# Three real products for a complex one in all four frequency classes of a fused spectral filter and feed-forward kernel, with two butterfly buffers placed in the tags of later ones

## The chip, the cores and the metric

The kernel runs on one core of one Trainium2 chip. The metric is the device time of one execution in microseconds, as the median of several runs. A profiled execution gives the page and the trace that are read here; it has a time of its own.

## The reference, cut to what matters

```python
def reference(A_x, A_w_r, A_w_i, B_x, B_w1, B_w2):
    xn = _layernorm(A_x)                       # (1, 2048, 1024)
    X  = rfft2(xn)                             # 2048 x 513, complex
    s  = irfft2(X * (A_w_r + 1j * A_w_i))      # the spectral filter
    h  = silu(xn @ B_w1)                       # 1024 -> 3584
    g  = silu(h @ B_w2)                        # 3584 -> 1024
    return A_x + s * g
```

All inputs and the output are fp32. The feed-forward part is by far the larger one in multiplications; the two-dimensional transform, the filter and the transform back run beside it.

## The kernel before, in words

**Numbers in two halves.** Every factor of a matmul is split into a high and a low fp16 half, and every product is made as three passes: high by high, high by low, low by high. VectorE and ScalarE make these halves: a ScalarE copy with a scale gives the high half, a VectorE `scalar_tensor_tensor` the low one.

**The big matmuls.** `mm1` (L457) makes one chunk of 128 hidden features by 512 rows with 24 matmuls of 512 columns. There are 112 such chunks. ScalarE takes each result out of PSUM with a SiLU (L475), and `hidden` (L481) splits four of them at a time into halves that go to DRAM. The second product is written as seven products of half size (`PRODUCTS`); its chunks are `mm2` (L545, 42 matmuls of up to 512 columns), eight for each of the seven. Results of both lie in the PSUM pool `pf`, which has four buffers of one bank.

**The transform beside it.** It is cut into pieces that are taken from a queue `bg` between the chunks:

- `fd_gen` (four classes c of rows): `fa_mat` transforms along the 1024 columns, `fa_evac` copies to SBUF, `bfly` makes butterflies on VectorE in tiles `E`, `EE`, `EO`, `DS`, `P` and `Q`. Then, in four steps j, a radix-4 step over the rows (tiles `Rb`, `Rd`, `Ro`) and a split into halves in a tile `Rs`, which goes to DRAM as `vd`. For the frequency classes in `THREE` the sum of real and imaginary part (`total`, tile `vt` in tag `E`) is split too and goes to DRAM as `vs`.
- `f_gen` (16 units u; q = u // 4 is the frequency class, j = u % 4 the block of 128 columns): `mat` finishes the transform along the rows with the tables `kq`. For a class that is not in `THREE` it makes four groups of 9 matmuls into one PSUM tile `fx`: three passes of one matmul with 256 columns (L1001) and two with 128 (L1002, L1003). For a class in `THREE` it makes 36 matmuls with 128 columns (L994) into two PSUM tiles: one group multiplies the sum from `vs`, two multiply the real and the imaginary part from `vd`. `copy` then moves one part to SBUF on ScalarE (L1027, one copy into tile `xc`; or L1024, two copies, each laid out twice, into tile `xo` in tag `T1`). For a class in `THREE` two VectorE additions (L1056) join the three products. After that every unit is alike: butterflies `xb`, `xd`, `X`, the product with the weights `wq` (tiles `T1`, `T2`), `yb`, `yd`, `Z`, a split into `zq`, and a store to `zd`.
- `i_gen` (four classes, in the order 1, 3, 0, 2) makes the transform back; its results (`s`, for the last class `rows`) are used by the last steps of the second product.

**PSUM for the transform.** `fa`, `fx`, `iu` and `id` share the pool `pt`, tag `ft`, which has two buffers of two banks each.

**What sets the order.** The program writes the order of each engine's work by hand. After each chunk `after` runs the evacuations that are due (`settle`), delayed stores (`tick`), and `work`, which takes pieces from the queues: weights (`wq`), maxima (`xq`), and the transform (`bg`). A piece of `bg` is taken only while a running estimate of VectorE's time, made from the shapes of the instructions, is no more than `LEAD` = 1.0 us ahead of the same estimate for TensorE. So more VectorE work in `bg` moves later pieces to later chunks. A generator that yields `PAUSE` waits for the next chunk. The last four chunks of `mm1` take nothing from `bg` (`hold`), and when 15 chunks are left `f_job`, which ends the forward transform and opens the pool of `f_gen`, is finished in any case (L1604 to L1607).

**Queues.** Loads and stores are issued from the queue of SyncE (SP), in program order; `load_h` of the second product and the later tables `kq` from ScalarE's queue; the adding loads of `w2` (L424) and the first table from GpSimd's.

The lines of the change:

```python
THREE = (2, 3)                                                              # L28
room = ap.tile([128, 2048 + 256 * len(THREE)], F16, ..., tag="Rs", bufs=2)  # L882
total[j] = ap.tile([128, len(THREE), 128], F32, ..., tag="E", bufs=1)       # L907
load_s(u + 2)                                                               # L1061
```

## Time and profile before

| | |
|---|---|
| median of 3 runs | 1225.4 us (1224.5 to 1226.07) |
| profiled execution, its own time | 1228.22 us |
| its span | 1226.4 us |
| TensorE, VectorE, ScalarE busy | 99%, 82%, 40% of the span |
| instructions | 19138 |
| moved by DMA | 299.98 MB |

The span runs from the first to the last instruction; the own time is 1.8 us longer. In the rows that follow, PE is TensorE's matmuls, PEld its weight loads, DVE is VectorE, ACT ScalarE, POOL GpSimd, and SPq the queue of SyncE. A matmul's duration runs from its start to its modelled end and overlaps with that of the next one, so its cost is read from the distance between starts. The stages can be told by time: the forward transform runs to about 532 us, the 16 units of the filter from 552 to 843 us, `mm2` from 636 us to the end, and the transform back from 880 to 1172 us.

### The profile page before, as it was taken

What the parts mean: (1) busy time and instruction counts of PE and PEld (TensorE: products, weight loads), DVE (VectorE), ACT (ScalarE), POOL (GpSimd) and SP (SyncE); (2) the same over time, 40 slices, a digit from 0 to 9 for tenths busy, and PEclk for the clock granted to TensorE, in tenths of its full rate; (3) what the DMA queues carried; (4) which work ended last, traced back from release to release, by engine and by line L of the source; (5) the groups of instructions that cost most, each with busy time, mean ns of one, the idle gap of its engine ahead of it and who ended that gap; (6) DMA issues with size and microseconds to landing.
All of it is one profiled execution on the core that took longest, in us unless ns stands there. A gap on an engine that the chain in (4) does not pass through costs nothing.

```text
span 1226.4 us, 19138 instructions
## 1 busy us (share of the span) xinstructions
PE 1213.9 (99%) x6992; PEld 616.3 (50%) x6992; DVE 1004.1 (82%) x2007; ACT 494.7 (40%) x670; POOL 137.0 (11%) x255
## 2 busy tenths in 40 slices
PE   8999999999999999999999999999999999999998
PEld 5544445445444444445445555544555555455545
DVE  7778997898798798868968989895378976897766
ACT  6775553455375654434433222131132322333212
POOL 3320000002000000201101121142101111000000
PEclk9999999999999999999999999999999999999999
DMA  8887585747678978479998999987979999997677
GB/s 251 184 195 188 164 256 178 211 132 211 187 257 270 315 242 273 146 245 212 174 294 289 256 256 231 313 227 230 287 188 322 268 344 295 320 368 244 234 246 278
DMA packets 285055, 299.98 MB, mean 245 GB/s; under 512 B 48928, under 2 KB 211744, under 8 KB 284576
## 3 DMA queue, kind: packets, MB, share of 16 engines
q1 hardware_dynamic: 264944, 239.95, 67.1%
q10 hardware_dynamic: 15840, 50.67, 11.9%
q0 software_dynamic: 4176, 8.13, 3.6%
q8 instruction: 55, 0.90, 0.3%
q14 instruction: 40, 0.33, 0.1%
HBM read 188.05 MB, written 104.35 MB: 238 GB/s over the span
## 4 chain that ended last, share of the span: by engine, by line
PE 69%; DMA 10%; DVE 10%; ACT 3%; issue 2%; SPq 1%; POOL 0%; ACTq 0%; DVEq 0%; POOLq 0%
PE pa L466 33%; PE pb L549 10%; PE pb L550 10%; PE pb L551 10%; DMA zd<-zq 2%; PE id L1371 2%; DMA ht<-hd_dif 2%; DMA wq<-in_A_w_i_dram 1%; ACT xp L750 1%; DMA jr<-ws 1%; DMA jr<-in_B_w_dram 1%; PE iu L1289 1%; DMA ws<-wd 1%; PE iu L1281 1%; DVE wd L383 1%
## 5 line engine op out<-in xcount | busy, mean ns | idle before, releaser
L466 PE MATMUL pa<-xnT,w 128*128 128x512 f16 x2688 | 584.4, 379 | 1.3 <-ACT w L257 0.7
L466 PEld LDWEIGHTS <-w 128*128 128x128 f16 x2688 | 261.2, 98 | 312.5 <-issue 1.2
L549 PE MATMUL pb<-w,ht 128*128 128x512 f16 (+2 forms) x812 | 301.1, 373 | 0.0
L550 PE MATMUL pb<-w,ht 128*128 128x512 f16 (+2 forms) x812 | 301.0, 372 | 0.0
L551 PE MATMUL pb<-w,ht 128*128 128x512 f16 (+2 forms) x812 | 300.8, 372 | 0.0
L551 PEld LDWEIGHTS <-ht 128*128 128x128 f16 x812 | 79.6, 98 | 91.4 <-issue 0.8
L549 PEld LDWEIGHTS <-ht 128*128 128x128 f16 x812 | 79.8, 98 | 87.2 <-issue 0.8
L550 PEld LDWEIGHTS <-ht 128*128 128x128 f16 x812 | 79.6, 98 | 87.1 <-issue 0.6
L475 ACT ACTIVATE h<-pa,s 128x512 f32<-128x512 f32 x112 | 75.5, 677 | 76.7 <-PE pa L466 59.5
L257 ACT ACTIVATE w<-jr,sc 128x512 f16<-128x512 f32 x98 | 68.5, 714 | 76.1 <-DMA jr<-in_B_w_dram 57.2
L260 DVE SCALAR_TENSOR_TENSOR w<-jr,sc,w 128x512 f16<-128x512 f32 x98 | 71.9, 744 | 17.9 <-ACT w L257 17.8
L257 ACT ACTIVATE hosum<-hr,hs 128x1536 f16<-128x1536 f32 x28 | 44.0, 1572 | 87.4 <-DVE hr L505 37.5
L260 DVE SCALAR_TENSOR_TENSOR hoone<-h,hs,hoone 128x2048 f16<-128x2048 f32 x28 | 65.6, 2342 | 6.9 <-ACT hoone L257 6.9
L257 ACT ACTIVATE hoone<-h,hs 128x2048 f16<-128x2048 f32 x28 | 55.9, 1995 | 29.3 <-issue 11.8
L260 DVE SCALAR_TENSOR_TENSOR hosum<-hr,hs,hosum 128x1536 f16<-128x1536 f32 x28 | 50.7, 1811 | 1.4 <-ACT hosum L257 1.4
L504 DVE TENSOR_TENSOR hr<-h 128x1024 f32<-128x1024 f32 x28 | 34.1, 1219 | 21.3 <-ACT h L475 21.3
L257 ACT ACTIVATE w<-w1r,rs 128x1024 f16<-128x1024 f32 x28 | 31.9, 1143 | 37.5 <-DVE w L260 24.3
L424 POOL DMA_DIRECT2D jr<-in_B_w_dram x28 | 24.4, 948 | 181.5 <-DMA jr<-in_B_w_dram 43.7
L642 ACT ACTIVATE pl<-pl,c 128x512 f32<-128x512 f32 (+2 forms) x28 | 17.7, 656 | 66.3 <-DVE pl L618 36.5
L1033 ACT ACTIVATE zq<-Z,zs 128x1024 f16<-128x1024 f32 x16 | 18.4, 1148 | 58.5 <-DVE Z L1124 28.9
L1124 POOL TENSOR_TENSOR Z<-yb 128x32 f32<-128x32 f32 x32 | 15.9, 517 | 209.9 <-DVE yb L1103 209.9
L260 DVE SCALAR_TENSOR_TENSOR w<-w1r,rs,w 128x1024 f16<-128x1024 f32 x28 | 35.6, 1273 | 2.3 <-ACT w L257 2.2
(240 smaller groups left out, 1571.5 us busy)
## 6 DMA issues: line engine op xcount, KB each, us to landing
w1r<-in_B_w_dram SPq DMA_DIRECT2D x28, 512.0 KB, 6.7
hd_sum<-hosum SPq DMA_DIRECT2D x56, 256.0 KB, 2.9
hd_one<-hoone SPq DMA_DIRECT2D x56, 256.0 KB, 4.3
hd_dif<-hoone SPq DMA_DIRECT2D x56, 256.0 KB, 4.5
w2m<-in_B_w_dram SPq DMA_DIRECT2D x28, 512.0 KB, 6.1
ht<-hd_dif ACTq DMA_DIRECT2D x32, 448.0 KB, 8.1
jr<-in_B_w_dram SPq DMA_DIRECT2D x56, 256.0 KB, 7.7
ht<-hd_sum ACTq DMA_DIRECT2D x32, 448.0 KB, 5.5
```

The costliest lines, as they stand in the source:

```text
L257: nc.scalar.activation(hi, raw, AF.Copy, scale=scale)
L260: nc.vector.scalar_tensor_tensor(lo, raw, scale, hi, op0=OP.mult, op1=OP.subtract)
L424: nc.gpsimd.dma_start(raw[n], w2_block(*todo[n], 1), accum_op=OP.add)
L466: nc.tensor.matmul(ps, w[:, wh, d], xt[:, xh, d], start=(n == 0), stop=(n == 23))
L475: nc.scalar.activation(hq[:, 2 * (c % 2) + f % 2], ps, AF.Silu, scale=s1[:, f:f + 1])
L504: tt(sums[:, 0:2], hq[:, 0::2], hq[:, 1::2], op=OP.subtract)
L549: nc.tensor.matmul(ps, hh[:, 0], w[:, 0], start=first, stop=False)
L550: nc.tensor.matmul(ps, hh[:, 0], w[:, 1], start=False, stop=False)
L551: nc.tensor.matmul(ps, hh[:, 1], w[:, 0], start=False, stop=last)
L642: nc.scalar.activation(o, o, AF.Silu, scale=c2)
L1033: nc.scalar.activation(zqs[q][:, 0, :, 16 * j:16 * j + 16], zs_[u], AF.Copy, scale=zs)
L1371: nc.tensor.matmul(ps[:, g, cols], us[g][:, uh, 4 * r + p], C["ci"][:, ch, g, r, cols], start=(r == 0 and n == 0), stop=(r == 1 and n == 2 ...
```

## The change

`THREE` becomes (0, 1, 2, 3), so that classes 0 and 1 (units 0 to 7) are made in the way that classes 2 and 3 were. What follows from the constant: the tables of classes 0 and 1 hold cos and two sums instead of sines and cosines (the same size); `total` has four classes instead of two in each of the 16 steps of the forward transform, its two halves are 512 elements per partition instead of 256, and each store of `vs` has 256 KB instead of 128; `Rs` has 3072 fp16 elements per partition instead of 2560, in two buffers. Units 0 to 7 load `vs` too, and the first two of these loads are written out ahead of the loop. The tile `xc` of the plain form is no longer made; `vs` of the filter uses its tag. The butterfly tiles `P` and `Q` lose tags of their own (1040 bytes per partition each) and lie in the tags `Rb` and `Rd` (2048 bytes each), which the radix-4 step uses later in the same class.

```diff
-THREE = (2, 3)
+THREE = (0, 1, 2, 3)
...
             tt(ds[:, 1], o[:, 1], o[:, 3], op=OP.add)
-            pp = ap.tile([128, 4, 65], F32, name=f"P{c}_{p}", tag="P", bufs=1)
+            pp = ap.tile([128, 4, 65], F32, name=f"P{c}_{p}", tag="Rb", bufs=1)
             tt(pp[:, 0:4:3], o[:, 0], o[:, 2, ::-1], op=OP.add)
             tt(pp[:, 2:0:-1], o[:, 0], o[:, 2, ::-1], op=OP.subtract)
-            qq = ap.tile([128, 4, 65], F32, name=f"Q{c}_{p}", tag="Q", bufs=1)
+            qq = ap.tile([128, 4, 65], F32, name=f"Q{c}_{p}", tag="Rd", bufs=1)
...
         load_k(0)
         yield PAUSE
         load_v(0)
+        load_s(0)
         load_w(0)
         yield PAUSE
         yield PAUSE
         load_v(1)
+        load_s(1)
         load_w(1)
         load_k(1)
```

## The prediction

> **What bounds the kernel now.** I read the page's first part, then the waits of TensorE, then the order in time of the matmuls around the change, then the groups by shape and the busy time by stage.
>
> ```profile
> span 1226.4 us, 19138 instructions
> PE 1213.9 (99%) x6992; PEld 616.3 (50%) x6992; DVE 1004.1 (82%) x2007; ACT 494.7 (40%) x670; POOL 137.0 (11%) x255
> ```
>
> PE is busy but for 12.5 us. Its whole list of waits, with the total, the times and the longest, is this:
>
> ```profile
> PE tp L759 <- ACT x L750: 2.1, 3, 1.2
> PE fa L803 <- ACT L L813: 1.9, 1, 1.9
> PE eps L1161 <- POOL edge L1154: 1.1, 1, 1.1
> PE spin L1545 <- POOL ones L1537: 1.0, 1, 1.0
> PE pa L466 <- ACT w L257: 0.7, 1, 0.7
> PE pa L466 <- DMA xnT<-xs: 0.6, 1, 0.6
> PE tp L759 <- DVE xnT L767: 0.3, 1, 0.3
> ```
>
> These are 7.7 us in an execution of 1226.4 us, most of the rest lies before the first and after the last matmul, and no `fx` (the filter's product) and no `pb` (the second product) is in the list. PE could still be called busy while its instructions only overlap, so the starts must be looked at. The timeline of PE around unit 0, in the old form, and around unit 8, in the form that the change gives to all:
>
> ```profile
> 552.59 0.27 PE L1001 MATMUL fx<-vq,kq 128*128 128x256 f16 x1
> 552.70 0.22 PE L1002 MATMUL fx<-vq,kq 128*128 128x128 f16 x1
> 552.76 0.22 PE L1003 MATMUL fx<-vq,kq 128*128 128x128 f16 x1
> 552.81 0.27 PE L1001 MATMUL fx<-vq,kq 128*128 128x256 f16 x1
> ...
> 555.24 5.13 PE L466 MATMUL pa<-xnT,w 128*128 128x512 f16 x23
> ```
>
> ```profile
> 700.70 0.33 PE L994 MATMUL fx<-vs,kq 128*128 128x128 f16 x3
> 700.87 0.50 PE L994 MATMUL fx<-vq,kq 128*128 128x128 f16 x6
> ...
> 702.71 0.38 PE L549 MATMUL pb<-w,ht 128*128 128x512 f16 x1
> ```
>
> A matmul of 256 columns is followed after 0.11 us, one of 128 after 0.055. Nothing lies between the unit and the big matmuls on either side. PE streams without a hole here, so a column less is time less, as long as nobody makes PE wait.
>
> That is where the Trainium skill speaks against this change: Perfetto Trace Analysis, section Identifying the Most-Contended Engine, says that the share of matmul busy time is no measure of TensorE's headroom and that weight loads and the other engines' occupancy should be looked at. By that rule the 50% of PEld stand against DVE's 82%, DVE is the most contended engine, and the change moves work to it. The starts above say otherwise for PE, and a rival below holds what would follow if they didn't.
>
> **What is removed.** A unit in the old form takes 555.24 - 552.59 = 2.65 us of PE, in the new one 702.71 - 700.70 = 2.01 us: as many matmuls (36) and weight loads, but 4608 columns in place of 6144. The difference of 0.64 us times 8 units is **5.1 us of PE**. It is the only saving that counts. On ACT one copy of 592 ns goes per unit, for two others.
>
> **What is added.** The groups by shape, with busy time, mean ns and the idle time before:
>
> ```profile
> L994 PE MATMUL fx<-vq,kq 128*128 128x128 f16 x192 | 15.9, 219 | 0.0
> ...
> L1056 DVE TENSOR_TENSOR xo<-xo,fx 128x512 f32<-128x512 f32 x16 | 10.2, 674 | 0.0
> ...
> L1024 ACT ACTIVATE xo<-fx 128x512 f32<-128x512 f32 x16 | 8.7, 596 | 60.1 <-DVE yd L1104 49.8 <-DMA jr<-in_B_w_dram 10.2
> ...
> L909 DVE TENSOR_TENSOR vt<-Ro 128x256 f32<-128x256 f32 x16 | 6.8, 425 | 0.5
> ...
> L890 DVE SCALAR_TENSOR_TENSOR Rs<-vt,Rs 128x256 f16<-128x256 f32 x16 | 6.7, 418 | 0.0
> ...
> L884 ACT ACTIVATE Rs<-vt 128x256 f16<-128x256 f32 x16 | 6.5, 407 | 9.9 <-DVE vt L909 9.9
> ...
> L1027 ACT ACTIVATE xc<-fx 128x512 f32<-128x512 f32 x8 | 4.7, 592 | 13.6 <-PE fx L1003 8.1 <-issue 5.5
> ```
>
> *Forward transform.* L909, L890 and L884 go from 256 to 512 elements in each of 16 steps. No row has L909 at 512; L1056 has an addition of that size at 674 ns, 249 more, and I take the same step for L890 (its bounds: nothing and another 418). DVE: 16 x (0.249 + 0.249) = 8.0 us. ACT: at most to the 596 of L1024, 16 x 0.19 = 3.0 us.
>
> *Filter.* Units 0 to 7 get two additions each, 8 x 2 x 0.674 = 10.8 us of DVE, and on ACT 8 x (2 x 0.596 - 0.592) = 4.8 us. Together **18.8 us of DVE and 7.8 us of ACT**. Whether they cost anything depends on the room:
>
> ```profile
> 420.00:540.00 120.00, 120.00 (x578) 55.14 (x577) 106.73 (x213) 59.87 (x75) 10.86 (x9) 1.00 0.73 226
> 540.00:690.00 150.00, 150.00 (x872) 77.66 (x870) 123.03 (x188) 57.41 (x71) 13.12 (x26) 1.00 0.96 247
> 690.00:840.00 150.00, 148.84 (x920) 77.81 (x918) 138.60 (x252) 37.13 (x56) 38.95 (x87) 0.99 0.90 248
> ```
>
> The columns after the length are PE, PEld, DVE, ACT and POOL busy, the granted clock, DMA's share and GB/s. In 420 to 540 us DVE has 13.3 us free, in 540 to 690 us 27, against the 10.8 that units 0 to 7 bring there. And where there is no room, the estimate of DVE's time in the program's order puts the next piece of the transform behind a later chunk of big matmuls: PE's own work does not wait for it, the transform ends later. How much later may that be? Its last product and the first use of it by the second product:
>
> ```profile
> L633 DVE SCALAR_TENSOR_TENSOR pl<-rows,s_sc,pl x12: 345/614/752, 1200.8 to 1223.1; 128x512 f32<-128x512 f32 x6, 128x128 f32<-128x128 f32 x4, 128x256 f32<-128x256 f32 x2
> ...
> L1418 DVE SCALAR_TENSOR_TENSOR rows<-sk,spa x4: 283/288/292, 1154.3 to 1171.8; 128x128 f32<-128x128 f32 x4
> ```
>
> The first block of `rows` is ready at 1154.6 and used at 1200.8, the last at 1172.1 and used in the last 22 us. If all 18.8 us of DVE delayed it and PE came 5.1 us earlier, 24 of these 46 us would be gone. Cost: nothing. Without that cover every further microsecond would be paid in full, after the last matmul.
>
> *PSUM.* A unit in the new form takes both buffers of the pool that the transform's matmuls share, so the next unit's matmuls wait until L1056 has read the unit before. Units 8 to 15 run so already, and L994 has an idle time of 0.0. For units 0 to 7 I take 0; the nearest stall of this kind (PE at L803, waiting for ACT to clear that pool) is 1.9 us, once.
>
> *Loads and stores.* The issue rows (operation, count, size, median us from issue to landing):
>
> ```profile
> vs<-Rs SPq DMA_DIRECT2D x16, 128.0 KB, 5.4
> vs<-vs SPq DMA_DIRECT2D x8, 256.0 KB, 10.6
> ```
>
> 16 stores grow by 128 KB and 8 loads of 256 KB come new: 2.1 MB each way, 9 us of DMA traffic at the 226 to 247 GB/s of those stages. A load of unit u + 2 is issued a whole unit ahead, and must then wait only for the matmuls of unit u, like the `vq` load behind it; queued behind it on SP are the stores of hidden features and the loads of `w2`. The share of 0.96 between 540 and 690 us says that these will land later. PE waited for no `ht` and only 0.7 us for a weight, so I take 0, and up to 1 us if it gets twice as long.
>
> *The shared tags.* `P` and `Q` are written and read by DVE alone, and so are `Rb` and `Rd`. A new use stands behind the old one in the same queue: 0, and nothing to be gained.
>
> **Sum.** 5.1 us less on PE, all else covered: the profiled execution goes from 1228.22 to 1223.1 us (span 1221.3). The median of the runs is 2.8 us below the profiled one; the same saving puts it from 1225.4 to **1220.3 us**.
>
> **The rivals.** *A larger gain.* Other timing can take away the waits at L803 and L1161. The latter costs more than its 1.1 us. An undisturbed stretch of the chain that ended last, and PE's timeline right after that wait:
>
> ```profile
> 443.90 41.46 PE pa L466 x192
> ```
>
> ```profile
> 809.47 0.63 PE L550 MATMUL pb<-w,ht 128*128 128x512 f16 x1
> ...
> 812.03 0.52 PE L550 MATMUL pb<-w,ht 128*128 128x512 f16 x1
> ```
>
> In the first a matmul of 512 columns starts each 41.46 / 192 = 0.216 us. In the second six such steps take 2.56 us, 0.43 each, half that rate; 6 x 0.21 = 1.3 us are lost. With all three gone the time is 1220.3 - 1.9 - 1.1 - 1.3 = 1216.0 us. For it speaks only that the pieces shift; 12%.
>
> The Trainium skill, TensorE: Matmul & The Clock Gate, section What's actually happening, has the clock halved only after an idle window of about 3.4 us. By that rule a new wait shorter than that would cost its own length alone; by the rows above a wait of 1.1 us among small matmuls was followed by half the rate, so I count 1.3 us more.
>
> *No change.* The forward transform is where ACT and DVE already make PE wait. If each of the starts of its classes 1, 2 and 3 has a wait like the one of 1.9 us, 3.8 us come new, and with one spell of half the rate 5.1: 1225.4 us. The idle time of 13.3 us on DVE speaks against it. 14%, and another 1% for the case that units 0 to 7 run as before: the code branches on `THREE` alone, so I see no way to it.
>
> *Slower.* In the old form ACT's copy of a unit waits for PE (L1027: 8.1 us); in the new one it writes into the tag of `T1` and must wait until DVE has done `yd` of the unit before (L1024: 49.8 us, over 8 units 6.2 each). For units 8 to 15 ACT has little else to do. Units 1 to 4 run in the first product, where ACT's queue holds the SiLU behind that copy, and with it PE's four buffers. How near is that? ACT's timeline, and PE's:
>
> ```profile
> 612.58 0.67 ACT L475 ACTIVATE h<-pa,s 128x512 f32<-128x512 f32 x1
> ...
> 614.37 0.67 ACT L475 ACTIVATE h<-pa,s 128x512 f32<-128x512 f32 x1
> 615.19 0.69 ACT L475 ACTIVATE h<-pa,s 128x512 f32<-128x512 f32 x1 [0.15 <-PE pa L466]
> ```
>
> ```profile
> 604.63 17.64 PE L466 MATMUL pa<-xnT,w 128*128 128x512 f16 x81
> ```
>
> The third evacuation waited for the chunk that ended at 615.0, the second of the row from 604.63 on (24 matmuls, 5.18 us each chunk). So the first one, done at 613.25, is of the chunk before that row, and its buffer is wanted by the fourth chunk of it, at 604.63 + 3 x 5.18 = 620.2: 6.9 us to spare. A hold of 6.2 + 0.6 us by a copy just fits. The rival decides from 8.8 us a copy on, where four copies cost 1.9 us each and eat the 5.1 and 2.5 more. With 13 us for two of them it gives 1220.3 + 2 x 6.1 = 1232.5 us. Against it: right behind the copy ACT waits for a still later DVE instruction anyway (`Z`, for `zq`). 13%.
>
> *DVE as the bound* (what the page's rule above would lead to): the 18.8 us of DVE come on top and PE's saving turns into waiting, 1225.4 + 18.8 = 1244.2 us. Against it stand the 222 us in which DVE is idle, and PE's short list of waits. 6%.
>
> **How the numbers follow.** The forecast has 54%; its own range is one wait like L803's more or less, 1218.4 to 1222.2 us. 0.2% or 2.5 us is about what a measurement of this kernel can tell from no change. Faster by more: forecast and larger gain, 0.66. Within: 0.15. Slower: 0.13 + 0.06 = 0.19. The range reaches down to the larger gain, 1216.0, and up half the way from no change to the slower rival, (1225.4 + 1232.5) / 2 = 1229.0; left out are about half of that rival and the bound DVE, some 13%.
>
> **What would show it.** Right: L1001 to L1003 and L1027 gone, L994 with 576 matmuls in 16 units of 2.01 us, PE busy 5 us less, L1056 and L1024 with 32, DVE busy 17 to 20 us more, PE's waits still under 10 us in all, the last `rows` some 10 to 20 us later. Wrong: waits of PE at `pa` for L475 or at `fx` for L1056, half-rate spells, or `rows` later than their use.

## The result, and the profile after

The changed kernel takes **1243.87 us** (median of 5 runs, 1241.88 to 1246.09) where the kernel before takes 1226.07 (5 runs on the same chip): a ratio of **1.0136**, 95% interval 1.0119 to 1.0154. It is slower by some 17 us; 5 us faster was forecast. The profiled execution took 1241.88 us, its span is 1240.1 us, 13.7 more than the span before. It was the fastest of its five, and the profiled execution before lies 2.2 us above the 1226.07, so the two traces show 13.7 of the 17 us. The lines of the page that answer to those of before:

```profile
span 1240.1 us, 19155 instructions
PE 1213.8 (98%) x6992; PEld 615.0 (50%) x6992; DVE 1021.5 (82%) x2023; ACT 500.8 (40%) x678; POOL 133.5 (11%) x255
```

VectorE has 17.4 us more work and ScalarE 6.1, near the 18.8 and 7.8 expected. But PE busy is 1213.8 us as before, where 5 us less were expected. The groups by shape (busy, mean ns, idle before) say that the work itself is what the prediction counted:

```profile
L994 PE MATMUL fx<-vq,kq 128*128 128x128 f16 x384 | 32.6, 222 | 0.0
L994 PE MATMUL fx<-vs,kq 128*128 128x128 f16 x192 | 21.5, 221 | 4.2 <-DVE xo L1058 4.2
L1058 DVE TENSOR_TENSOR xo<-xo,fx 128x512 f32<-128x512 f32 x32 | 20.4, 678 | 7.0 <-ACT xo L1026 7.0
L1026 ACT ACTIVATE xo<-fx 128x512 f32<-128x512 f32 x32 | 17.4, 595 | 97.1 <-DVE yd L1106 97.1
L909 DVE TENSOR_TENSOR vt<-Ro 128x512 f32<-128x512 f32 x16 | 11.1, 692 | 0.5
```

There are 576 matmuls at L994 and none in the old form. What has grown is the time in which TensorE stands. Its waits (total, times, longest), those of 1 us and more after the start of the kernel:

```profile
PE iu L1291 <- DVE ub L1300: 4.7, 1, 4.7
PE fx L994 <- DVE xo L1058: 4.2, 2, 3.1
PE eps L1163 <- POOL edge L1156: 2.6, 1, 2.6
...
PE pb L549 <- DMA ht<-hd_dif: 1.6, 1, 1.6
PE fa L803 <- ACT L L813: 1.4, 1, 1.4
PE pa L466 <- ACT h L475: 1.2, 2, 1.0
```

In the list of before there was none of `iu`, `fx` or `pb`, and `eps` had 1.1 us. And by stage (PE, PEld, DVE, ACT, POOL busy, granted clock, DMA share, GB/s):

```profile
540.00:690.00 150.00, 147.78 (x870) 74.32 (x868) 119.38 (x179) 58.89 (x76) 14.88 (x23) 1.00 0.94 246
690.00:840.00 150.00, 142.59 (x865) 75.01 (x863) 133.27 (x242) 37.35 (x55) 20.01 (x50) 0.97 0.98 262
```

PE had 148.84 of 150 us in the second stage before and has 142.59 now. In the first, DVE is busy for 119.38 us where it was 123.03, although it has more to do: the work was not put into the idle time that was counted for it, but moved behind it.

**A balance.** For this and the runs below I worked out from all 6992 matmuls of a trace where TensorE's time goes. Each gets the distance that its shape keeps in undisturbed stretches (0.216 us for 512 columns, 0.109 for 256, 0.056 for 128, small ones in proportion, four times that in fp32). What the next one starts later than that is lost, be it a wait or half the rate; some 6 us of the span lie ahead of the first and after the last matmul. The executions in the table lie up to 3 us from the median of their kernel, so it accounts for their own spans. In us:

| kernel (profiled execution) | matmuls' own time | lost 0–540 | 540–700 | 700–870 | 870–end | span |
|---|---|---|---|---|---|---|
| before | 1208.0 | 7.5 | 0.0 | 4.7 | 0.4 | 1226.4 |
| after | 1202.9 | 6.1 | 2.6 | 14.6 | 8.2 | 1240.1 |
| forward part alone | 1208.0 | 6.3 | 0.3 | 8.9 | 0.4 | 1229.9 |
| products alone | 1202.9 | 6.8 | 0.0 | 7.9 | 5.9 | 1229.4 |
| old work, new order | 1208.0 | 6.7 | 0.0 | 4.3 | 11.3 | 1236.3 |
| new work, old order | 1202.9 | 7.5 | 11.9 | 12.3 | 0.4 | 1240.8 |
| products, old order | 1202.9 | 6.1 | 7.3 | 8.4 | 0.4 | 1231.1 |
| short products, one buffer | 1202.9 | 6.6 | 2.9 | 10.4 | 0.4 | 1229.1 |

The matmuls' own time falls by the 5.1 us, from 1208.0 to 1202.9, as it must with these distances and the new shapes. Against it stand 9.9 us more lost between 700 and 870 us, 7.8 after that and 2.6 before, less 1.4 at the start: 18.9 - 5.1 = 13.8, the 13.7 us of the spans but for rounding. PE busy hides the saving: at half the rate a matmul of 512 columns starts each 0.43 us in place of 0.216, still without a gap, so the longer stretch counts as busy throughout.

### The profile page after: what moved, and what is told of

Its sections match the earlier page's. It is cut to its first block, busy times and chain, and to the rows that moved or that the text cites. A ratio compares the mean times of both kernels' runs of the same rounds, so it can differ in the third digit from the quotient of the medians.

```text
span 1240.1 us, 19155 instructions
## 1 busy us (share of the span) xinstructions
PE 1213.8 (98%) x6992; PEld 615.0 (50%) x6992; DVE 1021.5 (82%) x2023; ACT 500.8 (40%) x678; POOL 133.5 (11%) x255
## 2 busy tenths in 40 slices
DMA packets 290303, 304.17 MB, mean 245 GB/s; under 512 B 49056, under 2 KB 215968, under 8 KB 289824
## 4 chain that ended last, share of the span: by engine, by line
PE 45%; DMA 21%; DVE 19%; ACT 4%; issue 4%; SPq 2%; ACTq 0%; DVEq 0%; POOL 0%; POOLq 0%
PE pa L466 27%; PE pb L549 5%; PE pb L551 5%; PE pb L550 5%; DMA jr<-in_B_w_dram 3%; DMA zd<-zq 2%; DMA ht<-hd_dif 2%; DVE w L260 2%; DVE Z L1126 2%; DMA jr<-ws 2%; PE id L1373 1%; DMA hd_dif<-hoone 1%; DMA vq<-vd 1%; DMA ht<-hd_sum_d 1%; ACT xp L750 1%
## 5 line engine op out<-in xcount | busy, mean ns | idle before, releaser
L475 ACT ACTIVATE h<-pa,s 128x512 f32<-128x512 f32 x112 | 75.1, 675 | 46.0 <-PE pa L466 34.6
L257 ACT ACTIVATE hoone<-h,hs 128x2048 f16<-128x2048 f32 x28 | 55.9, 1996 | 38.1 <-DVE h L509 14.5
L1026 ACT ACTIVATE xo<-fx 128x512 f32<-128x512 f32 x32 | 17.4, 595 | 97.1 <-DVE yd L1106 97.1
L642 ACT ACTIVATE pl<-pl,c 128x512 f32<-128x512 f32 (+2 forms) x28 | 17.4, 654 | 77.9 <-DVE pl L618 46.0
L994 PEld LDWEIGHTS <-kq 128*128 128x128 f16 x576 | 34.2, 99 | 8.4 <-issue 3.4
```

Source lines behind the costliest of these rows:

```text
L257: nc.scalar.activation(hi, raw, AF.Copy, scale=scale)
L475: nc.scalar.activation(hq[:, 2 * (c % 2) + f % 2], ps, AF.Silu, scale=s1[:, f:f + 1])
L642: nc.scalar.activation(o, o, AF.Silu, scale=c2)
L994: nc.tensor.matmul(ps[:, i, 128 * g:128 * g + 128], k[:, c, kh, g], src[:, vh], start=(n == 0), stop=(n == 2))
```

## The experiments

Every ratio is to runs of the kernel before on the same chip, with its 95% interval. The experiments ran on five chips, where the kernel before takes 1226.6 to 1229.3 us, so times from different chips are compared by ratio.

**The parts, each alone.**

*The forward part alone*: all four sums are made and stored, units 0 to 7 stay in the old form.

```diff
-THREE = (2, 3)
+THREE = (0, 1, 2, 3)
+FORM = (2, 3)      # stands for THREE in f_gen and in the tables
```

> The forward transform makes and stores all four sums, with P and Q in the shared tags, and the filter's units 0 to 7 stay in the old form. Added by the groups of before: 8 us of DVE, 3 us of ACT, 2.1 MB of stores; PE saves nothing. If the forward part is harmless, as I forecast, the time is that of before within 2.5 us, PE's waits stay at about 8 us in all and unit 0 comes some 4 to 7 us later. If lateness alone is what costs (the transform falls behind the four chunks that take nothing from the queue, and its sums then miss their use by the second product), this alone brings a part of it: 3 to 8 us slower, with waits of PE after 640 us only.

Measured: 1233.64 us (10 runs), ratio 1.0046 (1.0028 to 1.0064). DVE has 8.5 us more. The last sum of the forward part is made 4 us later and unit 15 comes 2 us later; the loss is in 700 to 870 us, where the wait at `eps` is 3.1 us and half-rate matmuls follow.

*The filter alone*: the mirror of it (`THREE = (2, 3)`, `FORM = (0, 1, 2, 3)`, units 0 to 7 read the sums of classes 2 and 3).

> The forward transform stays as before (two sums) and units 0 to 7 take the new form; what they load as sums are those of classes 2 and 3, so the products of classes 0 and 1 are not the reference's, and the work of units 0 to 7 is that of the change. PE saves 5.1 us; added are 10.8 us of DVE, 4.8 us of ACT and 2.1 MB of loads. If the cost is made at the units (PE waits for the two PSUM buffers until DVE has read them, ACT's copies wait for yd), nearly all of the change's 17 us stay: 9 to 17 us slower than before. If the loss is lateness that both parts build up, it is smaller: between 5 us faster and 6 us slower.

Measured: 1238.37 us (4 runs), ratio 1.0079 (1.0051 to 1.0106). TensorE waits 6.1 us for `ub`, 5.7 for `ht`, 3.3 for `jr`. Both parts cost, and 0.46% + 0.79% is about the whole.

*VectorE's work alone*: the old products, but `xb` and `xd` are made twice in units 0 to 7.

```diff
+            if u < 8:
+                tt(b.rearrange("m c r k -> m c (r k)"), pv, cpy, op=OP.add)
+                tt(d.rearrange("m c r k -> m c (r k)"), pv, cpy, op=OP.subtract)
```

> Before, with the two instructions that make xb and xd run twice in units 0 to 7, with the same result: 10.8 us of DVE more, of the size and at the place of the change's additions; PE, ACT, PSUM and DMA as before. If DVE's load is what costs, the units come later by about as much as in the changed kernel (unit 15 some 15 to 29 us later) and the time rises by 8 to 20 us. If the hold of PSUM or of ACT costs, the time rises by under 4 us.

Measured: 1237.29 us (7 runs), ratio 1.0081 (1.0051 to 1.0110), for 9.2 us more of DVE. So work added to DVE in these units is not free: the price is about its face value. It is not the price of the work alone, though. The written order counts the work and moves with it: in TensorE's sequence unit 15 now stands behind 3423 matmuls of `mm1` and `mm2`, one chunk more than the 3381 of before.

*The additions, taken out of the changed kernel*, but for one column of 128; the rest of these sums is left out of the result.

```diff
-                    tt(cpy[:, half], cpy[:, half], planes, op=OP.add)
+                    w_ = slice(0, 128 if q > 1 else 1)
+                    tt(cpy[:, half, :, :, w_], cpy[:, half, :, :, w_], planes[..., w_], op=OP.add)
```

> The changed kernel, but the two additions at L1058 take one column of 128 in units 0 to 7 (so the rest of these sums is left out of the computation). TensorE's and ScalarE's work, the forward part and the transfers stay as changed; VectorE's work falls by some 9 to 10 us of the 18.8 added. Theory A (each us that VectorE gets to do ahead of the last unit makes the transform later and comes back as waits of TensorE): 1243.9 less about 10 us, 1233 to 1235, with unit 15 some 12 us earlier and no wait for ub over 2 us. Rival B (the waits come of the changed form itself: two banks held by ScalarE's copy and the shared buffers): the time stays at 1240 or more.

Measured: 1236.41 us (6 runs), ratio 1.0052 (1.0038 to 1.0066). DVE has 8.3 us less than the changed kernel and the time falls by 1.0136 - 1.0052 = 0.84%, 10 us. The same price from the other side, and again with another order: unit 15 stands behind 3444 matmuls, in the changed kernel behind 3486. But 6.4 us are left without the additions, so theory A is half the story.

*The products alone* (forward part of before, sums of classes 2 and 3 in place of those of classes 0 and 1, additions of one column; the values of units 0 to 7 are left out):

> TensorE's part of the change with next to none of VectorE's: forward part as before the change, units 0 to 7 in three products with the stored sums of classes 2 and 3 in place of their own, and their additions of one column alone (so these units' values are left out of the computation). Theory A: TensorE's 5.1 us are kept nearly whole, 1226.6 less 5.1 is 1221.5, so 1220 to 1223, with waits of TensorE as in the kernel before (8 us). Rival B (the form, its copies by ScalarE or its loads cost something of themselves): 1225 or more.

Measured: 1232.37 us (11 runs), ratio 1.0024 (1.0013 to 1.0035). This was the surprise: 5.1 us of TensorE's work taken away, 1.3 us of DVE's added, and the time is longer. The theory "DVE's work costs, TensorE's saving counts" fell with it. Not all else is equal: ScalarE has 4.0 us more, eight loads of 256 KB come new, and unit 15 stands 63 matmuls, a chunk and a half, later in the order. Runs below take these apart.

**Lateness.**

*The transform later, without more work*: six pauses ahead of unit 8 (`if u == 8: for _ in range(6): yield PAUSE`) in the kernel before.

> Before, with six more pauses ahead of unit 8: no work added on any engine, the second half of the filter and the transform back come some 25 to 30 us later, as in the changed kernel. If lateness alone costs, PE waits 4 to 7 us in the second product's fifth part (DVE held by a reload of sums just stored) and perhaps more at the edge product: 5 to 10 us slower. If load and not lateness costs, the time is that of before within 3 us.

Measured: 1256.94 us (4 runs), ratio 1.0220 (1.0198 to 1.0242). Unit 15 comes 24 us later and TensorE waits 12.3 and 6.4 us for `ub`. Lateness by itself can cost more than the whole change. Here even the cover at the end is used up: the instruction that makes the last of `rows` starts at 1236.1 us and one that uses `rows` stands right behind it at 1236.3, and the span goes on for 13.6 us after the last matmul where it is 4.9 in the other runs. How lateness comes to cost ahead of the end, the changed kernel shows, in the timelines of DVE, of SyncE's queue, and of TensorE:

```profile
1041.97 0.28 DVE L1420 SCALAR_TENSOR_TENSOR s<-sk,spa 128x128 f32<-128x128 f32 x1
...
1060.47 0.75 DVE L633 SCALAR_TENSOR_TENSOR pl<-fs,s_sc,pl 128x512 f32<-128x512 f32 x1 [8.39 <-DMA fs<-sd]
...
1076.56 0.68 DVE L1300 TENSOR_TENSOR ub<-iu,uc 128x512 f32<-128x512 f32 x1
```

```profile
1046.40 0.61 SPq L1433 DMA_DIRECT2D sd<-s  x1
1055.04 0.32 SPq L566 DMA_DIRECT2D fs<-sd  x1
...
1056.24 0.43 SPq L566 DMA_DIRECT2D fs<-sd  x1
```

```profile
1077.30 0.94 PE L1291 MATMUL iu<-kk,zt 128*128 128x129 f16 x7 [4.68 <-DVE ub L1300]
```

The second sum `s` of class 3 is made by 1042.3 us. Its store is issued at 1046.4 and lands at 1055.0, the loads `fs` are issued only then, and the second of them lands at 1060.45. VectorE has come to the instruction that reads `fs` by 1052.1. It stands 8.39 us at the head of its queue until the round trip is done, and the next stage of the transform back (`ub`) stands behind it, and TensorE behind that. In the kernel before, the same sum is made at 1000.8 and the same instruction starts at 1045.6, without a wait.

*The reload finished one step later*:

```diff
+            if t_ is None:
+                t_ = rows_for(c, p, h, H["p"], (("fs", 3), ("fx", 2)))
+                return lambda: lambda: finish_out(tag, c, p, h, o, *(v[:, cols] for v in t_), cols)
```

> The changed kernel, but where an output chunk has to load stored sums again only when it is finished, the finishing is put one step of the queue later, so that VectorE does not stand at its head until the load has landed. Nothing of the computation is left out. Theory A (late sums, a reload that holds VectorE's queue, TensorE waiting for ub at L1300): the wait of TensorE's iu for ub falls from 4.7 us to under 1.5 us, the time lost after 1060 us from 6.8 to 1 or 2 us, and the time from 1243.9 to about 1238. Rival B (VectorE simply has too much to do there, the reload is only the instruction that happens to stand first): the wait for ub stays over 3 us and the time within 2 us of 1243.9.

Measured: 1245.36 us (4 runs), ratio 1.0147 (1.0120 to 1.0175): no gain, and TensorE's wait for `ub` is 7.3 us, as rival B has it. One step was not enough:

```profile
1074.10 0.75 DVE L633 SCALAR_TENSOR_TENSOR pl<-fs,s_sc,pl 128x512 f32<-128x512 f32 x1 [6.64 <-DMA fs<-sd]
...
1079.65 0.69 DVE L606 TENSOR_TENSOR pl<-pl,pb 128x512 f32<-128x512 f32 x1 [4.07 <-DMA pl<-pd]
```

VectorE stands idle for these 6.64 and 4.07 us, so it is a load that holds it, as theory A has it, and not too much work; but the remedy only moved the hold.

*The edge products one step later* (a second `yield 1` ahead of `eps` in `edge_gen` and one more `next(B["edge"], None)` at the end of `f_gen`):

> The changed kernel, but the small edge products (tile eps) are issued one step later, so that GpSimd's edge tile has longer to come. Nothing of the computation is left out. Theory A (TensorE stops 2.6 us at eps and then runs at half rate for some us; kernel before: the same place, smaller): the wait for edge goes, the time lost between 700 and 870 us falls from 14.6 to about 7 us, and the time from 1243.9 to about 1237. Rival B (what stands behind is late as well, and the wait only moves to the next tile): a new wait of 2 us or more within 30 us of the place, and the time within 2 us of 1243.9.

Measured: 1247.03 us (4 runs), ratio 1.0160 (1.0139 to 1.0181). Rival B: the wait at `eps` is gone and others stand in its place.

```profile
PE iu L1293 <- DVE ub L1302: 7.0, 1, 7.0
PE fx L994 <- DVE xo L1058: 4.6, 2, 3.3
PE iu L1285 <- DMA jr<-in_B_w_dram: 4.2, 1, 4.2
PE pb L549 <- DMA ht<-hd_dif: 4.0, 1, 4.0
```

*Held back for one chunk, not four* (`hold[0] = left < 1`):

> The changed kernel, but the transform is held back only for the last chunk of the first product instead of for its last four. Nothing of the computation is left out. Theory A (of the 29 us by which the units of the transform are late at unit 15, one whole unit, some 13 us, is lost because one unit fewer starts ahead of the hold): yb of unit 2 comes back from 651 to about 625 us, unit 15 from 862 to about 845, the sums of class 3 to 1020 to 1050, the wait for ub after 1060 us falls to 2 us or less, and the time to about 1235 to 1238. Rival B (the units that run in the last four chunks hold up the evacuations there, for which the hold was made): TensorE waits 5 us or more for evacuations between 590 and 650 us, and the time is 1244 or more.

Measured: 1242.89 us (4 runs), ratio 1.0135 (1.0114 to 1.0157): no difference. The unit lost is real, though. `yb` of units 2 and 15 in the kernel before, in the changed one, and here:

```profile
605.01 0.69 DVE L1103 TENSOR_TENSOR yb<-T 128x512 f32<-128x512 f32 x1
...
832.82 0.72 DVE L1103 TENSOR_TENSOR yb<-T 128x512 f32<-128x512 f32 x1
```

```profile
651.02 0.69 DVE L1105 TENSOR_TENSOR yb<-T 128x512 f32<-128x512 f32 x1
...
861.71 0.69 DVE L1105 TENSOR_TENSOR yb<-T 128x512 f32<-128x512 f32 x1
```

```profile
623.74 0.69 DVE L1105 TENSOR_TENSOR yb<-T 128x512 f32<-128x512 f32 x1
...
851.73 0.72 DVE L1105 TENSOR_TENSOR yb<-T 128x512 f32<-128x512 f32 x1
```

In the changed kernel unit 2 falls behind the four chunks in which nothing is taken from `bg`. Without that hold unit 15 is 10 us earlier and the wait for `ub` 2.8 us in place of 4.7, but `eps` waits 5.0 us in place of 2.6, and `fx` 4.2 as before, now in one piece. Waits move about; their sum hardly changes.

*The copy `xo` into the buffers of `X`*:

```diff
-                cps[u] = bp.tile([128, 2, 2, 2, 128], F32, name=f"xo{u}", tag="T1", bufs=1)
+                cps[u] = bp.tile([128, 2, 2, 2, 128], F32, name=f"xo{u}", tag="X", bufs=2)
```

> The changed kernel, but the copy xo of a butterfly goes into the two buffers of X and not into the one that it shares with yd of the unit before, so that ScalarE's copy no longer waits for VectorE's yd (97.1 us of waiting in 32 copies). Nothing of the computation is left out. Theory A (ScalarE standing at that copy delays what is queued behind it, and with it the units): the wait of TensorE's fx for xo at L1058 falls from 4.2 to under 1.5 us, the time lost between 540 and 870 us from 17.2 to 10 to 13 us, unit 15 is 5 to 10 us earlier, and the time is about 1236 to 1240. Rival B (the buffer of X is free no earlier than that of yd, or ScalarE's wait delays nobody): the copies wait about as long, for X, and the time stays within 2 us of 1243.9.

Measured: 1246.02 us (4 runs), ratio 1.0154 (1.0131 to 1.0177). The copies waited 47.6 us in all instead of 97.1, and nothing came of it: rival B, ScalarE's standing there is not what costs.

**The work and the order apart.** The order of the pieces is written from estimates made of the instructions, so a change of the work changes the order too. Putting the two clocks back or forward by hand parts them.

*The additions not counted* (`clock["dve"] -= 0.66 if q < 2 else 0` after each addition):

> The changed kernel, but the written order is made as if the additions of units 0 to 7 cost VectorE nothing (the planner's clock is put back by the 0.66 us that it counts for each of the 16); every instruction is still there. Nothing of the computation is left out. Theory A (VectorE itself is what the units wait for between 650 and 870 us; the order only follows it): the units come no more than 3 us earlier, TensorE waits longer for xo at L1058, and the time is 1243 to 1248. Rival B (the order makes the units late, VectorE could go faster): unit 15 is 8 us or more earlier, the wait for ub goes, and the time is 1236 to 1239.

Measured: 1237.66 us (5 runs), ratio 1.0072 (1.0059 to 1.0085). Unit 15's `yb` comes at 846.9 instead of 861.7, half of the loss is gone, and I had expected (theory A) that it would not be. So the order is a cost of its own; but is it the cost?

The run also prices the additions without their order. In its trace and in that of the run with additions of one column, TensorE's sequence of tiles is the same from first to last, and VectorE's but for three instructions. What differs is 8.1 us of VectorE's work, and for that the ratios are 1.0072 and 1.0052: 0.20%, 2.5 us, with intervals that overlap. Of the 0.84% by which the time fell with the additions, 0.64% went with the order.

*The old work in the new order.* With VectorE's clock moved forward by 1.315 us and TensorE's back by 0.647 for each of units 0 to 7, and VectorE's by 0.54 in each step of the forward part, TensorE's units stand at exactly the same places among the chunks as in the changed kernel:

> The kernel before with all its own work, but its units written in the order of the changed kernel: the planner's clocks are moved by what it counts for the change (VectorE 1.315 us more and TensorE 0.647 us less for each of units 0 to 7, VectorE 0.54 us more for each of the 16 steps of the forward part), so that TensorE's sequence of units among the chunks is that of the changed kernel. Nothing of the computation is left out. Theory A (what costs the time is the written order, which puts unit 15 six and a half half-chunks later): 12 to 20 us slower than the kernel before, with the same waits for ub after 1060 us. Rival B (VectorE's longer work itself costs the time, the order only follows it): at most 5 us slower than before.

Measured: 1238.92 us (6 runs), ratio 1.0091 (1.0068 to 1.0114), 11 us. Its loss is one wait after 1060 us, of the kind above:

```profile
PE iu L1293 <- DVE ub L1302: 8.7, 1, 8.7
```

*The new work in the old order*, with the opposite corrections:

> The changed kernel with all its work, but written in the order of the kernel before (the same clocks moved back by the same amounts), so that TensorE's sequence of units among the chunks is that of before. Nothing of the computation is left out. Theory A (the written order costs the time): unit 15 near 835 to 840 us, no wait for ub after 1060 us, TensorE waits for xo at L1058 of 3 to 6 us in all, and 1 us faster to 4 us slower than the kernel before. Rival B (VectorE's work costs it): VectorE is behind the order all through 650 to 830 us, TensorE waits 10 us or more for xo or yb there, and the time is 10 us or more above the kernel before.

Measured: 1242.19 us (6 runs), ratio 1.0118 (1.0095 to 1.0142). Nothing is late after 870 us; the bill comes earlier.

```profile
PE fx L995 <- DVE xo L1060: 9.9, 2, 8.8
PE eps L1166 <- POOL edge L1159: 4.0, 1, 4.0
```

Neither theory holds alone. The work must be somewhere: written early, TensorE waits for it at `fx`; written late, TensorE waits for the sums. The two ways cost 14.5 us (1.18%) and, with the lost unit, 16.7. What work costs depends on the order it is put into: in the old one, against the products alone (1.0042, below), the sums and additions cost 0.76%, 9.3 us for 16.3 us of VectorE; in the order of the additions of one column it was 2.5 us for 8.1.

*The same with the edge products later*:

> The changed kernel in the order of the kernel before, and the small edge products (tile eps) one step later, which by itself made the kernel before 0.26% faster. Nothing of the computation is left out. Theory A (the order and the edge wait are separate costs): 3 to 4 us faster than the changed kernel in the old order, so 4 us faster to equal with the kernel before. Rival B (the edge wait only moves to the next tile): equal with the changed kernel in the old order.

Measured: 1238.23 us (6 runs), ratio 1.0091 (1.0071 to 1.0110). Some 3 us better than without it, as theory A has it, but far from the kernel before.

**Why TensorE's saving does not show.**

*The products alone in the old order*:

> The new products with next to none of VectorE's work, as in the run of the products alone (units 0 to 7 with the sums of classes 2 and 3, their additions of one column: these units' values are left out), but in the order of the kernel before. Theory A (with the products alone the order put the units 1 to 4 half-chunks later, for its clock counts TensorE's shorter units, and that ate the saving): unit 15 at 828 to 834 us, no wait for ub, 4 to 6 us faster than the kernel before. Rival B (the new form costs something of itself, or TensorE waits for the transform as much longer as its work is shorter): within 2 us of the kernel before.

Measured: 1232.54 us (11 runs), ratio 1.0042 (1.0025 to 1.0059). A miss: with unit 15 at 835.8, and no wait for `ub`, it is still slower. TensorE waits 5.7 us for `xo` at 658 us and 2.8 at `eps`.

*The old products in both buffers of PSUM*: two of a unit's four blocks go to a second tile of tag `ft`, and VectorE lets it go by reading one column of it as it comes to the unit.

> The kernel before, its work and its order, but the products of a unit of classes 0 and 1 lie in both buffers of PSUM's tag ft (two of the four blocks in each) and the second is let go only as VectorE comes to the unit, by one read of a column: as the three-product form does it. Nothing of the computation is left out. Theory A (the form costs the second buffer: the products of the next unit can no longer be made ahead of VectorE's additions): TensorE waits 4 to 7 us for fx near 658 us, as in the products alone in the old order (5.7 us), and the time is 6 to 11 us above the kernel before. Rival B (the waits there come of TensorE's shorter work, which brings it to the place earlier): no wait of fx over 1 us, and within 2 us of the kernel before.

Measured: 1231.39 us (12 runs), ratio 1.0023 (1.0008 to 1.0038). There is no wait of `fx` at all, so theory A's place and size are wrong; 0.23% is above nothing all the same. A part of it can be the reads of a column, which add 1.4 us to VectorE.

*The short products in one buffer*, in the old order, without sums, additions or larger copies:

```diff
+                for r in range(2):
+                    for g in range(2 - r):
+                        for n, (kh, vh) in enumerate(((0, 0), (0, 1), (1, 0))):
+                            nc.tensor.matmul(ps[:, c, r], k[:, c, kh, r + g], v[:, c, vh, 128 * g:128 * g + 128], start=(n + g == 0), stop=(n == 2 and g + r == 1))
```

> The kernel before in its order, but the units of classes 0 and 1 do as many product columns as the three-product form (36 matmuls of 128 columns), with their results in one buffer of PSUM as before, with no sums, no additions and no larger copies (the values of these units are left out of the computation). Theory A (TensorE's saving is worth its full size where the second buffer stays free): 4 to 6 us faster than the kernel before, and no wait of fx. Rival B (shorter work of TensorE comes back as waits for the transform whatever the buffers are): within 2 us of the kernel before, with some 5 us more of waits at fx, eps or ub.

Measured: 1230.48 us (12 runs), ratio 1.0015 (1.0001 to 1.0030). Theory A is out: here nothing is added to any engine and TensorE does 5.1 us less, yet it is not faster. The order of both TensorE and VectorE is that of before, tile by tile, so this run shows where the saving goes. GpSimd and TensorE around the edge products, in the kernel before:

```profile
804.43 1.03 POOL L1124 TENSOR_TENSOR Z<-yb 128x32 f32<-128x32 f32 x2 [17.58 <-DVE yb L1103]
...
806.24 0.37 POOL L1154 COPY edge<-xsv 128x24 f32<-128x24 f32 x1
```

```profile
806.66 0.40 PE L1161 MATMUL eps<-edge,perm 128*128 128x24 f32 x2 [1.07 <-POOL edge L1154]
```

and in the kernel with the short products:

```profile
804.42 1.03 POOL L1124 TENSOR_TENSOR Z<-yb 128x32 f32<-128x32 f32 x2 [16.60 <-DVE yb L1103]
...
806.22 0.37 POOL L1154 COPY edge<-xsv 128x24 f32<-128x24 f32 x1
```

```profile
806.64 0.62 PE L1161 MATMUL eps<-edge,perm 128*128 128x24 f32 x2 [3.46 <-POOL edge L1154]
...
810.89 0.63 PE L550 MATMUL pb<-w,ht 128*128 128x512 f16 x1
...
816.01 0.46 PE L550 MATMUL pb<-w,ht 128*128 128x512 f16 x1
```

`eps` starts at 806.64 instead of 806.66. TensorE, with 5.1 us less to do, came to the same place and stood there: GpSimd's copies wait for its part of `Z`, that for VectorE's `yb` of unit 13, and the units come no faster because TensorE does. What TensorE saved it had lost again by then, 2.9 us at two starts of `fx` at 696 and 699 us (the trace puts them down to the load of `vs` and to ScalarE's `zq`) and the rest here.

What sets the time of `yb` is one more step back, in the timelines of ScalarE and VectorE, in the kernel before and then with the short products:

```profile
796.96 1.15 ACT L1033 ACTIVATE zq<-Z,zs 128x1024 f16<-128x1024 f32 x1 [9.74 <-DMA zd<-zq]
798.14 1.29 DVE L1038 SCALAR_TENSOR_TENSOR zq<-Z,zs,zq 128x1024 f16<-128x1024 f32 x1 [4.22 <-ACT zq L1033]
```

```profile
796.95 1.15 ACT L1033 ACTIVATE zq<-Z,zs 128x1024 f16<-128x1024 f32 x1 [8.78 <-DMA zd<-zq]
798.13 1.29 DVE L1038 SCALAR_TENSOR_TENSOR zq<-Z,zs,zq 128x1024 f16<-128x1024 f32 x1 [3.24 <-ACT zq L1033]
```

`zq` has one buffer, and the first unit of a class writes into it only when the stores `zd` of the class before have landed. Unit 12 of the run with short products was 0.95 us later than before at its `yb`; VectorE then stood for that landing in both. So it is not VectorE's speed that holds this place but the chain of the units, a store included, and that the two starts agree to 0.02 us is chance: the last stores landed at 796.86 and 796.85.

And TensorE lost more: after the longer wait it ran at half the rate until 816.0, where the short wait of before was followed by a spell that ended at 812.4. 2.9 + (10.4 - 4.7) - (7.5 - 6.6) - 5.1 = 2.6 us longer, where the spans differ by 2.7.

*The kernel before, with the edge products one step later*:

> The kernel before, but with the small edge products (tile eps) one step later. Nothing of the computation is left out. Theory A (in the kernel before the 4.7 us between 800 and 820 us hang on nothing but this wait, for there is slack behind it): about 4 us faster, 1222 to 1224. Rival B (TensorE's waits only move, as they do in the changed kernel): within 2 us of 1226.6.

Measured: 1225.44 us (9 runs) beside 1229.32, ratio 0.9974 (0.9962 to 0.9986). This is the one version that beats both kernels. In its profiled execution, at 1229.01 us the slowest of the nine, `eps` no longer waits, and a load does:

```profile
PE pb L549 <- DMA ht<-hd_dif: 2.7, 2, 2.5
```

The short products with the edge products later, where a part of the 5.1 us should show if this reading is right, were not tried, nor was a second buffer for `zq`.

## Why the prediction was wrong, point by point

- *TensorE's work, 5.1 us less*: right, 5.1. That it is **time** was wrong, and this is the first step that failed: "PE streams without a hole here, so a column less is time less, as long as nobody makes PE wait". The starts around units 0 and 8 were free of holes, but 106 us after unit 8 stood the wait of `eps` for `edge`, quoted in the prediction with its half-rate matmuls. It was counted as a loss that might go away. It says that TensorE reaches that point before the transform does, so a microsecond saved ahead of it is spent waiting there, as long as the transform comes no earlier. The short products show it: 5.1 us less to do, the starts of `fx` and `eps` held up by about that much more, and the start of `eps` at 806.64 in place of 806.66.
- *VectorE's 18.8 us*: 17.4 measured. "Cost: nothing" was wrong, the second step that failed: 8 to 9 us of them in the units cost 10 us, from both sides (1.0081 for work added, 0.84% for work removed). The larger part of that is the later order that the work brings with it: the new order cost 11 us without the work, the additions 2.5 us without a change of order, and work and products together 14.5 us in the old order. The prediction did name that order, and took it for harmless: "PE's own work does not wait for it". It does, at `eps`, `fx` and `ub`. The cover was read from the row with room (540 to 690 us, 27 us idle); the next row, 138.60 of 150 us, had hardly any, and the units are a chain through both. The written order did not put the work into the idle time either.
- *How much later*: unit 15 was to be at most 18.8 us later; it was 28.9, because a unit fell behind the hold (without the hold it is 18.9). And the margin was looked at for the last class alone:

```profile
L633 DVE SCALAR_TENSOR_TENSOR pl<-rows,s_sc,pl x12: 344/615/752, 1216.9 to 1236.8; 128x512 f32<-128x512 f32 x6, 128x128 f32<-128x128 f32 x4, 128x256 f32<-128x256 f32 x2
...
L1420 DVE SCALAR_TENSOR_TENSOR rows<-sk,spa x4: 284/285/285, 1187.0 to 1212.4; 128x128 f32<-128x128 f32 x4
```

The last `rows` are done at 1212.7 instead of 1172.1, 41 us later, and used from 1216.9 on: that margin just held. Class 3, wanted from 1052 us on, had none left, and paid: 8.39 us of VectorE, 4.7 us of TensorE.
- *PSUM, 0*: too low. `fx` waits 4.2 us in two places, longest 3.1. The chain at the longer one, in the timelines of VectorE, ScalarE and TensorE:

```profile
703.07 0.69 DVE L1106 TENSOR_TENSOR yd<-T 128x512 f32<-128x512 f32 x1
...
706.27 1.27 DVE L1058 TENSOR_TENSOR xo<-xo,fx 128x512 f32<-128x512 f32 x2
```

```profile
703.85 1.08 ACT L1026 ACTIVATE xo<-fx 128x512 f32<-128x512 f32 x2 [4.45 <-DVE yd L1106]
```

```profile
707.00 0.33 PE L994 MATMUL fx<-vs,kq 128*128 128x128 f16 x3 [3.07 <-DVE xo L1058]
```

`yd` of one unit, the next unit's copy that waited for it, the first of that unit's additions, and only then the products after it. A unit that holds both buffers lets the next products start only after all that. Old products in both buffers cost 0.23%, the reads of a column included; why the products alone in the old order waited 5.7 us at 658 us and neither half of them did there stays open.
- *Loads, 0 to 1*: 1.6 us for one `ht`, up to 5.7 in other runs. A size. The traffic was also counted for one direction only: 304.17 MB were moved in place of 299.98, and 4.2 MB at 226 to 247 GB/s are 17 to 19 us, not 9.
- *The slower rival* (ScalarE's copy holds the SiLU): the wait for L475 came, 1.2 us in all. The copies waited 97.1 us in 16 units, 6.1 a unit, as the 6.2 read before, and moving them elsewhere gained nothing. Not the cause.
- *No change*: no new wait came in the forward part. The one at L803 is 1.4 us, and before 540 us 6.1 us are lost where it was 7.5. *A larger gain*: it needed the wait at `eps` to go away, and that grew from 1.1 to 2.6 us.
- *DVE as the bound*, 1244.2 us, given 6%: the direction of its mechanism is right, TensorE's saving turned into waiting. That the number is right to 0.3 us is luck: the sum put all of VectorE's work on top, and the runs show 14.5 us for all the work in the old order and 11 us for the new order without it. VectorE needn't be busy all the time for the saving to be lost; it is enough that TensorE waits for the units' chain. The Trainium skill's rule (Perfetto Trace Analysis, Identifying the Most-Contended Engine), that matmul busy time is no good measure of how close TensorE is to its limit, bears out in one way here: PE busy did not fall by the 5.1 us that were saved. In the kernel before it misled little, for the matmuls' own time of 1208.0 us is 98.5% of the span and PE busy read 99%.
- The range ended at 1229.0 because the two slower cases were given 19% together. The trace had what was needed to weigh them: 138.60 of 150 us of DVE and the wait at `eps` in one stage.

## What to carry to other kernels

A wait of the busiest engine, however short, marks a place where another chain arrives last. Work saved on that engine ahead of the place can be worth nothing, as the 5.1 us were here, and work added to that chain, or an order that brings it later, can cost time however much idle time the other engines show; so look for the next such place behind the work that you mean to save, before you count the saving. Where a program writes its order from estimates, a change of cost is also a change of order: hold the order fixed to see which of the two you measure, and check the margin of every consumer, not of the last one only.

## What was not expected of the hardware

The length of a half-rate spell. In the kernel before, a wait of 1.07 us and small fp32 matmuls (eighteen in the trace, of 24 and 8 columns) were followed by full-size matmuls 0.43 us apart until 812.4; after a wait of 3.46 us at the same place the spell lasted to 816.0, and it began with the small matmuls themselves. The extra loss was larger than the wait that caused it: 6 us beside 3.46. The granted clock in the traces says how long the spells are: it is 0.5 from 808.9 to 812.3 us in the kernel before and from 805.9 to 816.2 with the short products, 3.41 and 10.24 us. Up to the last matmul, every spell recorded in the traces of this case lasts 3.41 us or two, three or four times that. So the loss comes in steps. It does not simply grow with the wait: in the new work in the old order TensorE stood 8.8 us at `fx`, until 663.1, with the clock at 0.5 from 657.2 to 667.4, so more than half of that spell fell into the wait and only about 4 us of matmuls were slow.

The Trainium skill (TensorE: Matmul & The Clock Gate, What's actually happening) ties the halved clock to an idle window of about 3.4 us. The steps of 3.41 us agree with a window of that length. The waits fit less well: with the short products the clock fell 2.7 us after TensorE had stopped, and the 1.07 us of the kernel before do not make such a window, unless small matmuls count as idle, which no run here shows by itself.
